# Three weight units converted beside the attention scores with part of the sums on GpSimd, and a reordered stretch from the norms to the first products

## The chip, the cores and the metric

The kernel runs on one core of one Trainium2 chip. The metric is the device time of one execution, in microseconds (us). TensorE multiplies matrices, VectorE and ScalarE work on tiles in SBUF and PSUM, GpSimd works on tiles in SBUF, and SyncE issues the DMAs in the order in which the program lists them. Each engine runs its own instructions strictly in program order and waits for others through semaphores.

## The reference

Channel attention over 6016 tokens of 256 channels, and two feed-forward layers with a hidden size of 2048:

```python
qn = q / (norm(q, axis=tokens) + 1e-6);  kn = k / (norm(k, axis=tokens) + 1e-6)
s = kn.T @ qn / tau                      # 256 x 256, a sum over all 6016 tokens
a = softmax(s, axis=-1)                  # exp(s - max) / (sum + 1e-9)
x = v @ a                                # 6016 x 256
h = x @ w_in1;  x2 = (h * clip(h + 3, 0, 6) / 6) @ w_out1
h = x2 @ w_in2; out = (max(h, 0) ** 2) @ w_out2
```

The four weight matrices arrive as float64 and have to be turned into float32 on the chip.

## The kernel before

**Scores.** The tokens are 47 tiles of 128 rows, loaded as 24 groups (one tile, then two each) into a ring of eight buffers. For each tile `squares` lets ScalarE square q and k into a PSUM bank and VectorE add that to one of two running sums in SBUF, and `score` lets TensorE multiply k by q for the two halves of the 256 x 256 result. For the last ten tiles the second half is put off (`late`): six of those ten scores (`LATE_AT`) come behind the matmuls that finish the norms (`nrm`), the other four behind the broadcast of the reciprocal norms (`rq_ps`).

**Units.** A unit is 512 columns of float64 weights. `from_float64` converts it in five stages: `magnitude` (one ScalarE operation, L154), `sign` (one ScalarE operation, L157, and two VectorE operations, L158 and L159), `high` (VectorE, L162), `low` (VectorE, L167), and `done`, in which `split` lets ScalarE round the value to a high part (L123) and VectorE subtract that to get a low part (L125). All five VectorE operations have their operands in SBUF. Unit 0 of `w_in1` is converted beside the scores; unit 1 is begun ahead of `nrm` and finished in the chain that follows; the others (`order`) follow at places listed in `START` (a place is half a step, below; with k < `DENSE` the five stages stand at consecutive places).

**Chain.** From the norms on: `nrm`, square root, reciprocals, `rq_ps`, per half `softmax`, transposes (`transposed`), and then M1 = (softmax) @ w_in1, 512 columns at a time: `m1_half` are TensorE passes, `m1_out` writes high and low parts of the result as weights, `m1_keep` a float32 copy. `split_first` makes high and low parts of the first tokens of v. `keep_busy` are matmuls on constants whose result nobody reads.

**Steps and the rest.** 32 steps follow for the first 1024 tokens, each six passes for h (`product`), the activation (`first`) and six passes into the accumulators (`second`), with the remaining units, three more parts of M1 and preparations between them. From 154 us on, both layers run in a Strassen scheme whose order is a list of numbered places. Matmuls in full precision are three passes of high and low parts (`passes`, L310 to L312).

Of the kernel before, what the change touches and what calls it, by code (L numbers as in the profile page):

```python
# [8 lines left out]
F32 = mybir.dt.float32  # L9
F32R = mybir.dt.float32r  # L10
I32 = mybir.dt.int32
U32 = mybir.dt.uint32
AF = mybir.ActivationFunctionType
ALU = mybir.AluOpType
AX = mybir.AxisListType

P = 128
C = 256
# [3 lines left out]
KC = C // P  # L22
KF = DFF // P
WIDTHS = [512] * 5 + [448]
NP = len(WIDTHS)
WMAX = max(WIDTHS)
NU = KF // 2
GROUPS = [1] + [2] * 23
DEFER = 10
LATE_AT = 6  # L30
LAG = 2
AHEAD = 3
BUSY = (6, 2, 2, 3)
M1_LEAD = 3
EARLY = 12
TAU_AT = 20
EARLY_AT = {15: (0, 1), 16: (2,), 18: (3, 4)}


START = [-5, -3, 0, 3, 6] + [9 + 4 * k for k in range(9)]  # L40
DENSE = 5
SIGN = -(2 ** 31)
APART = 2.6
APART_FIRST = 3.2
# [2 lines left out]
B11, B21, T2, T3, T1, B22, T4 = range(7)  # L47
# [8 lines left out]
def attention_then_two_ffns(  # L56
# [30 lines left out]
    nc = tc.nc  # L87

    const = ctx.enter_context(tc.tile_pool(name="const", bufs=1))
    wpool = ctx.enter_context(tc.tile_pool(name="wpool", bufs=1))  # L90
    stage = ctx.enter_context(tc.tile_pool(name="stage", bufs=3))
    tpool = ctx.enter_context(tc.tile_pool(name="tpool", bufs=2))
    ops = ctx.enter_context(tc.tile_pool(name="ops", bufs=1))
# [7 lines left out]
    def bank(shape, name, tag=None):  # L101

        if tag is None:
            tag = "yxyq"[turn[0] % 4]
            turn[0] += 1
        return ps_h.tile(shape, F32, tag=tag, name=name, bufs=2 if tag == "y" else 1)
# [13 lines left out]
    def split(hi, lo, x, part=2, eng=nc.vector):  # L120

        if part != 1:
            nc.scalar.copy(hi, x)  # L123
        if part != 0:
            eng.tensor_tensor(out=lo, in0=x, in1=f32(hi), op=ALU.subtract)  # L125
# [47 lines left out]
    wi1, wo1 = {}, {}  # L173
# [4 lines left out]
    def unit(which, u, raw=None):  # L178

        name = f"{which}_{u}"  # L180
        raw = (slot(name) if raw is None else raw).bitcast(I32)
        if which == "wi1":
            c4, k = u // 2, u % 2
            nc.sync.dma_start(out=raw, in_=w_in1[:, k, c4 * 512:(c4 + 1) * 512].bitcast(I32))

            def done(x, part=2):
                if k == 0 and part != 1:
                    wi1[c4] = [
                        spare(2 * c4 + i, f"wi1{s}{c4}", F32R).rearrange("p (k f) -> p k f", k=KC)
                        for i, s in enumerate(("h", "l"))  # L190
                    ]
                split(wi1[c4][0][:, k, :], wi1[c4][1][:, k, :], x, part)
        else:
            nc.sync.dma_start(
                out=raw.rearrange("p (f d) -> p f d", f=2), in_=w_out1[:, 2 * u:2 * u + 2, :].bitcast(I32)
            )

            def done(x, part=2):
                if part != 1:
                    wo1[u] = wo_tile(u, "wo1_")  # L200
                split(wo1[u][:, 0, :], wo1[u][:, 1, :], x, part)

        return from_float64(raw.rearrange("p (d w) -> p d w", w=2), name, done)
# [72 lines left out]
    def small(n):  # L276
        where = next(i for i in range(len(used)) if used[i] + n <= 2 * WMAX)
        at = used[where]
        used[where] += n
        return scratch[where][:, at:at + n]  # L280

    def keep_busy(n, name):

        ps = bank([P, P], name)
        for _ in range(n):
            nc.tensor.matmul(ps, lhsT=ones, rhs=ones, start=True, stop=True)

    s_ps = [ps_acc.tile([P, C], F32, tag="acc", name=f"s{i}") for i in range(KC)]

    sums = [small(2 * C) for _ in range(2)]  # L290
    for x in sums:
        nc.vector.memset(x, 0.0)

    def squares(t, x):
        sq = bank([P, 2 * C], f"sq{t}")
        nc.scalar.activation(sq, x, AF.Square)
        nc.vector.tensor_tensor(out=sums[t % 2], in0=sq, in1=sums[t % 2], op=ALU.add)

    def score(t, x, i):
        nc.tensor.matmul(  # L300
# [13 lines left out]
    with tc.manual_schedule():  # L314
# [8 lines left out]
        pre = []  # L323
        t = 0
        for gi, n in enumerate(GROUPS):
            src = wpool.tile([P, 1024], F32, tag=f"wo{gi % NU}", name=f"qk{gi}")[:, :2 * n * C]
            nc.sync.dma_start(
                out=src.rearrange("p (t x c) -> p t x c", t=n, x=2), in_=qk[:, t:t + n, :, :]
            )
            if gi == EARLY:  # L330
                pre.append(unit("wi1", 0, raw1[0]))
            for st in EARLY_AT.get(gi, ()):
                pre[0][st]()
            if gi == TAU_AT:
                nc.sync.dma_start(out=tau_sb, in_=tau.to_broadcast([P, 1]))
                tq = small(4)
                nc.gpsimd.memset(tq, 1.0)
                nc.gpsimd.tensor_scalar(
                    out=tq[:, 2:4], in0=tq[:, 2:4], scalar1=tau_sb, scalar2=1.0, op0=ALU.mult, op1=ALU.mult
                )  # L340
            for j in range(n):
                x = src[:, j * 2 * C:(j + 1) * 2 * C]
                squares(t, x)
                score(t, x, 0)
                if t < NT - DEFER:
                    score(t, x, 1)
                else:
                    late.append((t, x, 1))
                t += 1
# [1 line left out]
        et = [hpool.tile([P, KC, C], F32R, tag="o", bufs=4, name=f"et{s}") for s in ("h", "l")]  # L351

        order = [
            ("wo1", 0), ("wi1", 2), ("wo1", 1), ("wi1", 3), ("wo1", 2), ("wi1", 4), ("wo1", 3), ("wi1", 5),
            ("wo1", 4), ("wi1", 6), ("wo1", 5), ("wi1", 7), ("wo1", 6), ("wo1", 7),
        ]
        loaded = []

        def feed():
            k = len(loaded)  # L360
            if k < len(order):
                which, u = order[k]
                loaded.append(unit(which, u, raw1[u] if which == "wi1" and u < len(raw1) else None))
# [4 lines left out]
            for k in range(KC):  # L368
                nc.sync.dma_start(out=raw[k][:, :, :w], in_=(vt[p] if j == 0 else x2_d[p])[:, 2 * k:2 * k + 2, :w])

        pre.append(unit("wi1", 1, raw1[1]))
        raw0 = [gpool.tile([P, 2, WMAX], F32, tag="g", name=f"v0_{k}") for k in range(KC)]
        load_x(0, 0, raw0)
        for _ in range(AHEAD):
            feed()


        for st in range(4):
            pre[1][st]()


        nrm = ps_acc.tile([P, 4], F32, tag="acc", name="nrm")
        for b in range(4):
            for m, x in enumerate(sums):
                nc.tensor.matmul(
                    nrm[:, b:b + 1], lhsT=x[:, b * P:(b + 1) * P], rhs=ones[:, 0:1], start=(m == 0), stop=(m == 1)
                )
# [3 lines left out]
        nc.vector.tensor_scalar_max(x2n, nrm, 1e-30)  # L391
        root = small(4)
        nc.scalar.activation(root, x2n, AF.Sqrt, scale=2.0 ** -10)
        pre[1][4](0)
        rec = small(4)
        nc.vector.reciprocal(rec, root)
        half = small(4)
# [5 lines left out]
        nc.vector.reciprocal(rnorm, norm)  # L403

        rq_ps = ps_acc.tile([P, C], F32, tag="acc", name="rq_ps")
        loaded[0][0]()
        for i in range(KC):
            diag = small(P)
            nc.vector.tensor_scalar(out=diag, in0=ident, scalar1=rnorm[:, i:i + 1], scalar2=None, op0=ALU.mult)
            nc.tensor.matmul(rq_ps[:, i * P:(i + 1) * P], lhsT=ones, rhs=diag, start=True, stop=True)  # L410
        for a in late[LATE_AT:]:
            score(*a)
        pre[1][4](1)
        loaded[0][1]()
        nc.scalar.activation(warm, ones[:, 0:1], AF.Exp)
        rq = small(C)
        nc.scalar.copy(rq, rq_ps)

# [24 lines left out]
        def row_sums(i, e, sm, et_ps):  # L443
            rs = const.tile([P, 1], F32, name=f"rs{i}")
            nc.vector.tensor_scalar_add(rs, sm, 1e-9)
            nc.vector.reciprocal(rs, rs)
            rsum.append(rs)
# [4 lines left out]
        def m1_half(c4, i, j):  # L452
            if j == 0:
                mps[c4, i] = bank([P, 512], f"mp{c4}_{i}")
            passes(mps[c4, i], [(
                [t[:, i, j * P:(j + 1) * P] for t in et], [t[:, j, :] for t in wi1[c4]],
            )], j == 0, j == KC - 1)
# [48 lines left out]
            hi, lo = (t[:, u, S1:, :] for t in wa1[c4])  # L506
            split(hi, lo, m1_st[c4][:, u, :, :], part, idle_first(c4 < 2))


        operands = {}  # L510
        raws = {}

        def operand(j, p, r):

            at = j * NP + p
            if r in (B11, B21) and at % 2:
                t = wpool.tile([P, 2, WMAX], F32R, tag=f"b{2 + r}", name=f"x{j}_{p}_{r}")
            elif r == T2 and at % 2:
                t = ops.tile([P, 2, WMAX], F32R, tag="opx", name=f"x{j}_{p}_{r}")
            else:  # L520
                t = ops.tile([P, 2, WMAX], F32R, tag=f"op{r}", name=f"x{j}_{p}_{r}")
            t = t[:, :, :WIDTHS[p]]
            operands[j, p, r] = [t[:, i, :] for i in range(2)]
            return operands[j, p, r]


        x0 = {}

        def split_first(k):
            w = WIDTHS[0]  # L530
            for n in range(2):
                hi, lo = x0[k, n] = operand(0, 0, ((B11, T3), (B21, B22))[k][n])
                split(hi, lo, raw0[k][:, n, :w])

        e0 = softmax(0)
        keep_busy(BUSY[1], "busy1")
        loaded[0][2]()
        transposed(0, *e0)
        e1 = softmax(1)
        loaded[0][3]()  # L540
        loaded[0][4](0)
        rest(0, *e0)
        loaded[0][4](1)
        feed()
        row_sums(0, *e0)
        keep_busy(BUSY[2], "busy2")
        m1_half(0, 0, 0)
        transposed(1, *e1)
        rest(1, *e1)
        row_sums(1, *e1)  # L550
        m1_half(0, 0, 1)
        for k in range(KC):
            split_first(k)
        loaded[1][0]()
        m1_out(0, 0)
        for j in range(KC):
            m1_half(0, 1, j)
        m1_out(0, 1)
        m1_keep(0)
        loaded[1][1]()  # L560
        loaded[1][2]()
        keep_busy(BUSY[3], "busy3")


        x2_d = [dram.tile([P, 4, WMAX], F32, name=f"x2d{p}") for p in range(NP)]
# [408 lines left out]
```

## Time and profile before

| | |
|---|---|
| time, median of 3 runs | 1046.49 us (1046.17 to 1046.52) |
| the profiled execution's own time | 1046.23 us |
| its span, first to last instruction | 1044.1 us |
| busy in the span | TensorE 1033.6, VectorE 863.0, ScalarE 665.6, GpSimd 29.9 us |

The span is 2.1 us shorter than the execution's time, the same execution seen from outside. Times in the rows below count from the start of the span. Matmuls overlap, so that TensorE's progress is read from the starts of its instructions rather than from their durations.

### The profile page before, as it was taken

How to read it: one execution, taken by the hardware profiler on the slowest of the kernel's cores; microseconds unless marked ns; L12 is line 12 of the kernel's file. 1: busy time of each engine (PE TensorE's matmuls, PEld its weight loads, DVE VectorE, ACT ScalarE, POOL GpSimd, SP SyncE). 2: the span in 40 equal slices, each digit the busy share in tenths (PEclk: the TensorE clock that was granted, in tenths of full speed). 3: DMA queues.
4: the chain of work that ended last, by engine and by line, in shares of the span. 5: the costliest groups of instructions: out<-in, count | busy, mean ns of one | idle time of the engine just before them, and what ended most of it. 6: DMA issues, size and time to landing. Idle time of an engine off the chain costs nothing.

```text
span 1044.1 us, 12995 instructions
## 1 busy us (share of the span) xinstructions
PE 1033.6 (99%) x4630; PEld 865.3 (83%) x4630; DVE 863.0 (83%) x1461; ACT 665.6 (64%) x1200; POOL 29.9 (3%) x33
## 2 busy tenths in 40 slices
PE   9999999999999999999999999999999999999998
PEld 8867787888888888888998888888888888888997
DVE  7899868889989989988987788778688678778765
ACT  7687777788878778777876455445455455445443
POOL 0012240000000000000000000000000000000000
PEclk9999999999999999999999999999999999999999
DMA  9911204003403402222665002002001100200100
GB/s 371 344 40 41 81 1 142 1 1 116 157 0 116 156 1 111 82 76 92 227 225 187 1 1 80 1 1 69 13 1 40 42 1 1 75 1 1 41 1 36
DMA packets 25936, 77.64 MB, mean 74 GB/s; under 512 B 2832, under 2 KB 4880, under 8 KB 25872
## 3 DMA queue, kind: packets, MB, share of 16 engines
q1 hardware_dynamic: 25872, 76.82, 21.0%
q8 instruction: 36, 0.59, 0.2%
q14 instruction: 28, 0.23, 0.1%
HBM read 52.95 MB, written 23.86 MB: 74 GB/s over the span
## 4 chain that ended last, share of the span: by engine, by line
PE 88%; DVE 7%; ACT 4%; issue 1%; DMA 1%; SPq 0%; ACTq 0%
PE acc L312 15%; PE acc L311 15%; PE acc L310 15%; PE y L310 7%; PE y L311 7%; PE y L312 7%; PE q L311 4%; PE q L310 4%; PE q L312 4%; PE s L300 3%; PE x L312 2%; PE x L310 2%; PE x L311 2%; DVE gs L125 2%; DVE g L630 1%
## 5 line engine op out<-in xcount | busy, mean ns | idle before, releaser
L125 DVE TENSOR_TENSOR gs<-g,gs 128x512 fp32r<-128x512 f32 (+1 forms) x384 | 260.4, 678 | 55.6 <-ACT gs L793 46.1
L312 PE MATMUL acc<-gs,wo 128*128 128x512 f32 (+1 forms) x768 | 296.8, 386 | 0.8 <-DVE gs L125 0.6
L310 PE MATMUL acc<-gs,wo 128*128 128x512 f32 (+1 forms) x768 | 296.2, 386 | 0.9 <-ACT gs L123 0.9
L311 PE MATMUL acc<-gs,wo 128*128 128x512 f32 (+1 forms) x768 | 295.9, 385 | 0.0
L793 ACT CAST gs<-g 128x512 fp32r<-128x512 f32 (+1 forms) x352 | 208.6, 613 | 31.0 <-DVE g L784 22.0
L312 PEld LDWEIGHTS acc<-gs,wo 128*128 128x128 f32 x768 | 144.2, 188 | 30.8 <-DVE gs L125 4.0
L310 PEld LDWEIGHTS acc<-gs,wo 128*128 128x128 f32 x768 | 144.2, 188 | 28.5 <-ACT gs L123 2.0
L311 PEld LDWEIGHTS acc<-gs,wo 128*128 128x128 f32 x768 | 144.2, 188 | 26.6
L766 ACT COPY se<-y 128x512 f32<-128x512 f32 (+1 forms) x88 | 50.7, 576 | 121.3 <-PE y L312 121.2
L770 DVE TENSOR_TENSOR h<-q,se 128x512 f32<-128x512 f32 (+1 forms) x88 | 59.5, 676 | 63.1 <-ACT se L766 62.6
L766 ACT COPY su<-y 128x512 f32<-128x512 f32 (+1 forms) x88 | 50.7, 576 | 87.1 <-PE y L312 76.4
L789 DVE SCALAR_TENSOR_TENSOR g<-h 128x512 f32<-128x512 f32 (+1 forms) x144 | 97.0, 673 | 0.0
L776 ACT ACTIVATE r<-h,three 128x512 f32<-128x512 f32 (+1 forms) x120 | 85.5, 713 | 8.6 <-DVE h L770 8.2
L784 DVE SCALAR_TENSOR_TENSOR g<-r,h 128x512 f32<-128x512 f32 (+1 forms) x120 | 80.6, 672 | 3.8 <-ACT r L776 3.8
L778 ACT ACTIVATE r<-y 128x512 f32<-128x512 f32 (+1 forms) x48 | 28.3, 590 | 62.7 <-PE y L312 62.7
L770 DVE TENSOR_TENSOR h<-q,su 128x512 f32<-128x512 f32 (+1 forms) x88 | 59.4, 675 | 1.4
L770 DVE TENSOR_TENSOR h<-x,sa 128x512 f32<-128x512 f32 (+1 forms) x88 | 59.1, 672 | 0.0
L766 ACT COPY sa<-y 128x512 f32<-128x512 f32 (+1 forms) x88 | 50.7, 576 | 6.8 <-PE y L312 0.7
L789 DVE SCALAR_TENSOR_TENSOR g<-y,r 128x512 f32<-128x512 f32 (+1 forms) x48 | 32.7, 681 | 23.7 <-ACT r L778 23.1
L300 PE MATMUL s<-qk 128*128 128x256 f32 x188 | 41.7, 381 | 0.8 <-DMA qk<-in_qk 0.8
L300 PEld LDWEIGHTS s<-qk 128*128 128x128 f32 x188 | 35.5, 191 | 6.1 <-DMA qk<-in_qk 1.5
L310 PE MATMUL y<-x,wa_0h 128*128 128x512 f32 (+1 forms) x88 | 34.0, 386 | 0.7 <-ACT se L766 0.7
(241 smaller groups left out, 1761.6 us busy)
## 6 DMA issues: line engine op xcount, KB each, us to landing
qk<-in_qk SPq DMA_DIRECT2D x23, 512.0 KB, 7.0
wo<-in_w_out SPq DMA_DIRECT2D x16, 512.0 KB, 5.2
wi<-in_w_in SPq DMA_DIRECT2D x10, 512.0 KB, 4.6
x2d<-o SPq DMA_DIRECT2D x20, 256.0 KB, 2.4
raw<-x2d SPq DMA_DIRECT2D x10, 512.0 KB, 5.6
out<-o SPq DMA_DIRECT2D x20, 256.0 KB, 2.2
raw<-in_vt SPq DMA_DIRECT2D x8, 512.0 KB, 5.9
wo2d<-wo2s SPq DMA_DIRECT2D x8, 512.0 KB, 2.9
```

The source lines that it names most:

```text
L125: eng.tensor_tensor(out=lo, in0=x, in1=f32(hi), op=ALU.subtract)
L300: nc.tensor.matmul(s_ps[i], lhsT=x[:, C + i * P:C + (i + 1) * P], rhs=x[:, :C], start=(t == 0), stop=(t == NT - 1))
L310: nc.tensor.matmul(ps, lhsT=ah, rhs=bh, start=first, stop=False, skip_group_check=more)
L311: nc.tensor.matmul(ps, lhsT=al, rhs=bh, start=False, stop=False, skip_group_check=more)
L312: nc.tensor.matmul(ps, lhsT=ah, rhs=bl, start=False, stop=last, skip_group_check=more)
L766: nc.scalar.copy(s[tag], s["y"])
L770: nc.vector.tensor_tensor(out=s[which], in0=s[ps], in1=s[tag], op=ALU.add)
L776: nc.scalar.activation(s["r" + which], h, AF.Relu, bias=three)
L778: nc.scalar.activation(s["r" + which], h, AF.Relu)
L784: nc.vector.scalar_tensor_tensor(out=g, in0=s["r" + which], scalar=6.0, in1=h, op0=ALU.min, op1=ALU.mult)
L789: nc.vector.scalar_tensor_tensor(out=g, in0=h, scalar=0.0, in1=r, op0=ALU.max, op1=ALU.mult)
L793: nc.scalar.copy(gs[which][0], s["g" + which])
```

## The change

- The ring for q and k has seven buffers and not eight (wo1 to wo7).
- Three units (0 and 1 of `w_in1`, 0 of `w_out1`) are loaded behind groups 6, 9 and 12 and converted at 3, 3, 4, 5 and 6 groups after their loads; before it was one, loaded behind group 12.
- Every third tile below 39 (1, 4, ..., 37: 13 tiles) is squared into SBUF and added to a third sum by GpSimd. At tile 41 VectorE adds the third sum to the first.
- `split_first(0)` stands ahead of `nrm`; `split_first(1)` is two halves between the softmax and M1. The table load for Exp stands right behind the square root; of the unit stages in the chain, only one `magnitude` is left. Five late scores stand ahead of `rq_ps` and five behind it.
- The transposes of the second half stand ahead of M1's first passes; the last `keep_busy` is gone; `order` and `START` are new.

```diff
-LATE_AT = 6
+LATE_AT = 5
-BUSY = (6, 2, 2, 3)
+BUSY = (6, 2, 2)
-EARLY = 12
+EARLY = ((6, "wi1", 0), (9, "wi1", 1), (12, "wo1", 0))
+EARLY_AT = (3, 3, 4, 5, 6)
-EARLY_AT = {15: (0, 1), 16: (2,), 18: (3, 4)}
+POOL_UNTIL = 39
+JOIN = 41
-START = [-5, -3, 0, 3, 6] + [9 + 4 * k for k in range(9)]
-DENSE = 5
+START = [-1, 2, 5, 8, 11, 14, 17, 22, 26, 30, 34, 39, 45]
+DENSE = 3
...
     def squares(t, x):
-        sq = bank([P, 2 * C], f"sq{t}")
-        nc.scalar.activation(sq, x, AF.Square)
-        nc.vector.tensor_tensor(out=sums[t % 2], in0=sq, in1=sums[t % 2], op=ALU.add)
+        if t % 3 == 1 and t < POOL_UNTIL:
+            sq = hpool.tile([P, 2 * C], F32, tag="r", name=f"sq{t}")
+            nc.scalar.activation(sq, x, AF.Square)
+            nc.gpsimd.tensor_tensor(out=sums[2], in0=sq, in1=sums[2], op=ALU.add)
+        else:
+            sq = bank([P, 2 * C], f"sq{t}")
+            nc.scalar.activation(sq, x, AF.Square)
+            nc.vector.tensor_tensor(out=sums[t % 2], in0=sq, in1=sums[t % 2], op=ALU.add)
+        if t == JOIN:
+            nc.vector.tensor_tensor(out=sums[0], in0=sums[2], in1=sums[0], op=ALU.add)
...
-            src = wpool.tile([P, 1024], F32, tag=f"wo{gi % NU}", name=f"qk{gi}")[:, :2 * n * C]
+            src = wpool.tile([P, 1024], F32, tag=f"wo{1 + gi % (NU - 1)}", name=f"qk{gi}")[:, :2 * n * C]
...
-            if gi == EARLY:
-                pre.append(unit("wi1", 0, raw1[0]))
-            for st in EARLY_AT.get(gi, ()):
-                pre[0][st]()
+            for i, (x, which, u) in enumerate(EARLY):
+                if gi == x:
+                    pre.append(unit(which, u, raw1[u] if which == "wi1" else None))
+                for st, after in enumerate(EARLY_AT):
+                    if gi == x + after:
+                        pre[i][st]()
...
-        pre.append(unit("wi1", 1, raw1[1]))
...
-        for st in range(4):
-            pre[1][st]()
+        split_first(0)
...
         nc.scalar.activation(root, x2n, AF.Sqrt, scale=2.0 ** -10)
-        pre[1][4](0)
+        nc.scalar.activation(warm, ones[:, 0:1], AF.Exp)
+        loaded[0][0]()
...
-        loaded[0][0]()
...
-        pre[1][4](1)
-        loaded[0][1]()
-        nc.scalar.activation(warm, ones[:, 0:1], AF.Exp)
...
         e0 = softmax(0)
         keep_busy(BUSY[1], "busy1")
-        loaded[0][2]()
         transposed(0, *e0)
         e1 = softmax(1)
-        loaded[0][3]()
-        loaded[0][4](0)
+        row_sums(0, *e0)
         rest(0, *e0)
-        loaded[0][4](1)
-        feed()
-        row_sums(0, *e0)
+        split_first(1, 0)
         keep_busy(BUSY[2], "busy2")
-        m1_half(0, 0, 0)
         transposed(1, *e1)
         rest(1, *e1)
         row_sums(1, *e1)
+        m1_half(0, 0, 0)
         m1_half(0, 0, 1)
-        for k in range(KC):
-            split_first(k)
-        loaded[1][0]()
+        split_first(1, 1)
         m1_out(0, 0)
         for j in range(KC):
             m1_half(0, 1, j)
         m1_out(0, 1)
         m1_keep(0)
-        loaded[1][1]()
-        loaded[1][2]()
-        keep_busy(BUSY[3], "busy3")
```

## Rows read from the trace of the kernel before

**Rows 1.** Windows: busy time and count of each engine, clock, DMA share, GB/s.
```profile
7.70:41.60 33.90, 33.90 (x159) 29.87 (x159) 30.77 (x52) 26.90 (x49) 0.70 (x1) 1.00 1.00 378
41.60:55.90 14.30, 12.86 (x72) 10.28 (x70) 11.60 (x32) 10.05 (x22) 0.00 (x0) 1.00 0.67 265
55.90:154.40 98.50, 96.25 (x407) 75.30 (x408) 84.48 (x139) 74.20 (x129) 25.69 (x21) 1.00 0.14 43
...
200.00:300.00 100.00, 100.00 (x442) 82.81 (x442) 92.04 (x160) 79.90 (x142) 0.00 (x0) 1.00 0.21 72
```

**Rows 2.** The chain that ended last, pieces: start, duration, what.
```profile
7.68 33.94 PE s L300 x156
...
45.41 1.28 ACT L415
...
46.91 0.27 ACT scratch L417
```

**Rows 3.** Timeline of the scores: start, duration, instruction, idle before and releaser.
```profile
20.23 0.60 ACT L296 ACTIVATE sq<-qk 128x512 f32<-128x512 f32 x1 [0.15 <-DMA qk<-in_qk]
22.70 0.60 ACT L296 ACTIVATE sq<-qk 128x512 f32<-128x512 f32 x1 [1.35 <-DMA qk<-in_qk]
25.39 0.66 ACT L154 ACTIVATE tbwi<-raw11h 128x512 f32<-128x512 f32 x1
25.94 0.68 ACT L157 ACTIVATE tywi<-raw11h 128x512 int32<-128x512 uint32 x1
26.17 0.42 DVE L158 TENSOR_SCALAR tawi<-raw11h 128x512 int32<-128x512 int32 x1
26.50 0.42 DVE L159 TENSOR_SCALAR tbwi<-tbwi 128x512 f32<-128x512 f32 x1
28.35 0.68 DVE L162 SCALAR_TENSOR_TENSOR tawi<-tbwi,tawi 128x512 int32<-128x512 int32 x1
28.95 0.68 DVE L297 TENSOR_TENSOR scratch<-sq,scratch 128x512 f32<-128x512 f32 x1
31.35 0.68 DVE L167 CUSTOM_DVE_ANT_0 tawi<-tawi,tywi 128x1024 uint16<-128x1024 uint16 x1
32.06 0.62 ACT L123 CAST wi1h<-tawi 128x512 fp32r<-128x512 f32 x1 [2.36 <-DVE tawi L167]
32.59 0.59 ACT L296 ACTIVATE sq<-qk 128x512 f32<-128x512 f32 x1
32.71 0.69 DVE L125 TENSOR_TENSOR wi1l<-tawi,wi1h 128x512 fp32r<-128x512 f32 x1 [0.69 <-ACT wi1h L123]
33.32 7.26 DVE L297 TENSOR_TENSOR scratch<-sq,scratch 128x512 f32<-128x512 f32 x12
```

**Rows 4.** Timeline later on, GpSimd (POOL) and VectorE (DVE) at the same time.
```profile
91.80 0.92 POOL L216 TENSOR_TENSOR m<-m 128x256 f32<-128x256 f32 x1
92.05 0.96 DVE L159 TENSOR_SCALAR tbwi<-tbwi 128x512 f32<-128x512 f32 x1
...
114.63 0.69 DVE L630 SCALAR_TENSOR_TENSOR g<-r,h 128x512 f32<-128x512 f32 x1 [0.90 <-ACT r L628]
114.84 1.30 POOL L125 TENSOR_TENSOR wa_1l<-m,wa_1h 128x512 fp32r<-128x512 f32 x1
115.24 1.46 DVE L167 CUSTOM_DVE_ANT_0 tawo<-tawo,tywo 128x1024 uint16<-128x1024 uint16 x1
```

**Rows 5.** Timeline from the norms to the first product.
```profile
41.24 1.97 PEld L385 LDWEIGHTS nrm<-both,scratch 128*128 128x128 f32 x16
...
45.84 0.61 PE L410 MATMUL rq_ps<-scratch,both 128*128 128x128 f32 x4
...
53.49 0.39 PE L312 MATMUL mp<-wi1l,eth 128*128 128x512 f32 x1
...
54.50 0.47 ACT L476 ACTIVATE wa_0h<-mp,rs 128x256 fp32r<-128x256 f32 x1
...
55.91 0.50 PE L311 MATMUL h<-x,wa_0l 128*128 128x512 f32 x1 [0.38 <-DVE wa_0l L478]
```

More of the change, by code (lines that the diff above doesn't have):

```diff
@@ L288, in attention_then_two_ffns @@
     s_ps = [ps_acc.tile([P, C], F32, tag="acc", name=f"s{i}") for i in range(KC)]
-    sums = [small(2 * C) for _ in range(2)]
+    sums = [small(2 * C) for _ in range(3)]
     for x in sums:
@@ L353, in attention_then_two_ffns @@
         order = [
-            ("wo1", 0), ("wi1", 2), ("wo1", 1), ("wi1", 3), ("wo1", 2), ("wi1", 4), ("wo1", 3), ("wi1", 5),
-            ("wo1", 4), ("wi1", 6), ("wo1", 5), ("wi1", 7), ("wo1", 6), ("wo1", 7),
+            ("wi1", 2), ("wi1", 3), ("wo1", 1), ("wo1", 2), ("wi1", 4), ("wi1", 5), ("wo1", 3), ("wo1", 4),
+            ("wi1", 6), ("wo1", 5), ("wi1", 7), ("wo1", 6), ("wo1", 7),
         ]
@@ L375, in attention_then_two_ffns, with operand, split_first @@
             feed()
-        for st in range(4):
-            pre[1][st]()
+        operands = {}
+        raws = {}
+        def operand(j, p, r):
+            at = j * NP + p
+            if r in (B11, B21) and at % 2:
+                t = wpool.tile([P, 2, WMAX], F32R, tag=f"b{2 + r}", name=f"x{j}_{p}_{r}")
+            elif r == T2 and at % 2:
+                t = ops.tile([P, 2, WMAX], F32R, tag="opx", name=f"x{j}_{p}_{r}")
+            else:
+                t = ops.tile([P, 2, WMAX], F32R, tag=f"op{r}", name=f"x{j}_{p}_{r}")
+            t = t[:, :, :WIDTHS[p]]
+            operands[j, p, r] = [t[:, i, :] for i in range(2)]
+            return operands[j, p, r]
+        x0 = {}
+        def split_first(k, *halves):
+            w = WIDTHS[0]
+            for n in halves or range(2):
+                hi, lo = x0[k, n] = operand(0, 0, ((B11, T3), (B21, B22))[k][n])
+                split(hi, lo, raw0[k][:, n, :w])
+        split_first(0)
         nrm = ps_acc.tile([P, 4], F32, tag="acc", name="nrm")
         for b in range(4):
-            for m, x in enumerate(sums):
+            for m, x in enumerate(sums[:2]):
                 nc.tensor.matmul(
@@ L507, in m1_sums_split @@
             split(hi, lo, m1_st[c4][:, u, :, :], part, idle_first(c4 < 2))
[L510 to L533, printed above, removed]
         e0 = softmax(0)
         keep_busy(BUSY[1], "busy1")
-        loaded[0][2]()
         transposed(0, *e0)
         e1 = softmax(1)
-        loaded[0][3]()
-        loaded[0][4](0)
+        row_sums(0, *e0)
         rest(0, *e0)
-        loaded[0][4](1)
-        feed()
-        row_sums(0, *e0)
+        split_first(1, 0)
         keep_busy(BUSY[2], "busy2")
-        m1_half(0, 0, 0)
         transposed(1, *e1)
```

## The prediction

> **What bounds the kernel now.** I first cut the span into four stretches by the windows view [rows 1]. During the scores (7.7 to 41.6 us) TensorE is busy throughout, and VectorE is busy for 30.8 of 33.9 us: two engines near their limit, TensorE just ahead. The chain of waits [rows 2] says the same: 156 score matmuls without a break, 33.94/156 = 0.2176 us apart. A tile is four of them, 0.87 us; each of the last ten, with half put off, is two, 0.435 us. From 41.6 to 55.9 us the chain goes through all engines in turn (table load, copy of `rq_ps`, and so on). In the steps, 55.9 to 154.4 us, 407 matmuls take 98.5 us; at the undisturbed spacing of 100/442 = 0.2262 us they need 92.1, so TensorE waits some 6.4 us there. From 200 us on nothing is missing [rows 1]; what follows the steps is only shifted. So I ask three things: do the scores still end on time, what does the chain save, and do the steps change?
>
> **Loads.** Groups 12 and 13 were first squared, after a wait for their load, at 20.23 and 22.70 us, with one unit's load between: 2.47 for two loads, 1.24 us per 512 KB [rows 3]. Counting back, group 7 had landed by 14.1; with a unit ahead of it 15.3, while TensorE wants its first tile (13) at 7.68 + 10 x 0.87 = 16.4. Group 10 comes at 20.2 against 21.6, group 13 at 25.2 against 26.8. The seventh-buffer ring issues the last group when tile 32 is scored, at 33.8; landings at 1.24 us per group put it at 37.7, and it is wanted at 40.7. The two loads more are thus hidden by the scores: 0, with at least 1.1 us of cover; without the cover up to 1 us.
>
> **The sums, by counting.** Spacings on VectorE [rows 3]: a sum 0.60 (28.35 to 28.95; twelve in 7.26), L158 0.33, L159 0.33, `high`, `low` and the low part 0.60 to 0.61 each, a unit 2.47. On ScalarE a magnitude 0.55, a sign 0.57, a rounding 0.53 (32.06 to 32.59); I take a square at 0.53 as well, the same size as the rounding. GpSimd's 13 adds remove 13 x 0.60 = 7.8 us from VectorE; the units add 2 x 2.47 plus the join 0.6, all beside the scores. But the help is spread over all tiles, and the units stand in groups 9 to 18. The sum of tile 17 starts at the earliest at 19.3: group 9 lands at 17.7, and its two squares stand behind a magnitude and a sign. From there VectorE owes 23 sums, 13.9, the join 0.6 and 6.75 of unit work (7.41 without the sign just done): 40.6 us if it never waits. `nrm` started at 41.24 [rows 5]. So 0.6 us may be lost.
>
> **The sums, with waits.** Two kinds of wait occur. In the old layout, ScalarE idled 2.36 us until `low` was done and VectorE 0.69 for the rounding [rows 3]; now ScalarE has a magnitude, a sign and two squares queued behind each rounding, and VectorE's sums need those squares. The second kind is in [rows 4]: L167 starts at 115.24, while GpSimd runs 114.84 to 116.14, and takes 1.46 in place of 0.68; L159 at 92.05 ends 0.29 after GpSimd and takes 0.96 in place of 0.42; but L630, which reads one operand from PSUM, takes 0.69 beside GpSimd. So I let VectorE's unit operations and GpSimd's adds exclude each other, first come first served, and leave the sums (PSUM and SBUF) undisturbed. An add is 1.30 us, the row of its size [rows 4].
>
> Laid out by hand in program order: tile 18's sum ends at 20.9. Unit 0: `high` to 21.5; `low` waits for the add of tile 19 until 22.8; the low part for that of tile 22 until 24.7; with the next sign and four sums this ends at 27.2. Unit 1: `high` meets the add of tile 25 (26.9 to 28.2), `low` that of 28 (28.8 to 30.1); ScalarE gets to round only at 30.8, so its next squares start at 32.4; this ends at 34.3. Unit 2: `high` meets the add of 31 (to 35.5), `low` that of 34 (to 37.4); 40.5. Three groups thus take 6.3 to 7.1 us where TensorE needs 5.2. Nine sums and the join follow, 6.05 us from 40.8: 46.9, so `nrm` is 5.7 late. Had `high` of unit 1 come 0.3 us sooner, it would have gone ahead of the add and the rest would end at 45.3, 4.1 late. Without any exclusion the same layout ends at 42.4, 1.2 late. I take the middle of the first two, **+4.9**; bounds 0 (the count above) and 5.7.
>
> [...]
>
> **The chain from `nrm` to the first product**, first on the old clock. Before, `rq_ps` was ready at 45.84 + 0.61 = 46.45, but ScalarE was in the table load (45.41 to 46.69) and the copy stands at 46.91 in the chain [rows 2, 5]. Now the table load runs 43.75 to 45.03 and the one magnitude ends at 45.7; five late scores end at 45.33, `rq_ps` is ready at 45.95, copied at 46.0: -0.8 for the first half. The second half needs the five other scores, 45.95 + 10 x 0.2176 plus drain = 48.3, so that it gains only about 0.3. Its exponential stands behind the first rounding of the transposes (49.0 to 49.35), so its transposes end at 50.55, and M1's twelve passes, without waits, at 50.55 + 12 x 0.2262 = 53.27; before it was 53.49 + 0.23 = 53.72 [rows 5]. Now comes the larger part: before, `m1_out` waited on ScalarE behind four roundings of v and a magnitude until 54.50, and the products got going at 55.91 - 0.23 = 55.68 [rows 5]. With two roundings ahead of the norms and two in gaps, `m1_out` runs at 52.1, its low part ends at 53.43, and the products start at 53.27, their second pass at 53.5. **-2.4**; bounds -0.5 (M1 alone) and -3. The roundings ahead of the square root cost nothing while `nrm` runs (1.97 us for 2 x 0.60 on VectorE, 2 x 0.53 on ScalarE). With `keep_busy` six matmuls go, in time in which TensorE waited anyway: 0.
>
> **Steps.** 13 units remain where 12 and the last two stages of a thirteenth did: sign and `high` more, 1.3 us of VectorE among 84.5 [rows 1]. Per step VectorE needs 1.3 for activation and low part and TensorE 12 x 0.2262 = 2.71, so a unit (2.47) per three places asks 1.3 + 1.65 per step, 0.2 too much; one per four places fits. The old order was dense up to place 13, the new one is lighter up to place 10 and dense to 22. I expect some 1 us less waiting at first and as much more afterwards: **0**, bounds -1.5 and +1.5.
>
> **Sum**, against the profiled execution: 1046.23 (span 1044.1 and 2.1 around it) + 4.9 - 2.4 + 0 = 1048.7. The median of the runs is 0.26 above that execution: **1049.0**.
>
> **Rivals.** (1) The exclusion costs next to nothing, since unit operations fall into GpSimd's gaps: `nrm` 1.2 late, 1046.49 + 1.2 - 2.4 = 1045.3. For it: GpSimd is idle half the time. Against: in [rows 4] both operations of a unit were blocked in full. (2) The sums end on time, TensorE ends the scores as before, and the chain's saving stands alone: 1044.1, or 1042.6 with the steps' lower bound. It needs VectorE to lose under 0.6 us in 21; from that point each microsecond lost is one on the end. (3) TensorE idles nearly 5 us ahead of `nrm`, longer than at any place of the old trace, and runs at half rate afterwards; five late scores ahead of `rq_ps` would then take 2.2 us more: 1051.2. [...]
>
> **How the numbers follow.** Forecast 0.48, on its own 1047.0 to 1050.2; rival 1 0.22; rival 2 0.15; rival 3 0.15. A measurement tells about 0.2% from no change, 2.1 us: 1044.4 to 1048.6 counts as the same. Of the forecast 0.33 lies above that and 0.15 within; rival 3 is slower; rival 1 is within, but for 0.03; rival 2 is faster. Faster 0.18, same 0.34, slower 0.48. The range 1043.8 to 1052.4 leaves out half of rival 2 and the top of rival 3, with the loads' extra microsecond.
>
> **What would show it.** Right: `nrm` starts near 46 us and not at 41.2, behind VectorE's sums; TensorE has a gap just ahead of it; VectorE's L162, L167 or L125 in 20 to 38 us are often 1.0 us and longer; the first product follows `nrm`'s start by 12.0 us and not 14.4; 98 to 99 us lie between it and the first Strassen pass. Wrong: `nrm` near 41 to 42 us; score matmuls with gaps that a load ends (then the ring is too short); or a first stretch of the steps with far less waiting than 6 us in all. What I trust least is whether each unit operation meets an add: a few tenths of shift in the squares change who comes first.

## The result: slower by 0.9%

The changed kernel takes 1056.03 us (median of 4 runs, 1054.28 to 1057.16), the kernel before 1046.51 in the same comparison: a ratio of 1.009, 95% interval 1.0078 to 1.0102. That is 9.5 us more, where 2.5 were forecast and the range ended at 1052.4. The profiled execution has a span of 1054.8 us, 10.7 more than before.

The windows view of the changed kernel, in the four stretches of [rows 1] (bounds moved to its own first product and its first Strassen pass):

```profile
7.70:41.60 33.90, 33.59 (x156) 29.56 (x156) 28.91 (x43) 27.61 (x51) 16.64 (x14) 1.00 0.99 387
41.60:60.20 18.60, 14.67 (x67) 12.44 (x65) 10.77 (x29) 9.04 (x20) 0.00 (x0) 0.82 0.47 193
60.20:165.20 105.00, 99.66 (x410) 77.70 (x409) 87.01 (x140) 74.67 (x129) 26.00 (x22) 0.97 0.13 41
165.20:1054.80 889.60, 884.72 (x3973) 744.89 (x3971) 732.92 (x1235) 551.27 (x996) 1.69 (x2) 1.00 0.18 62
```

The last stretch is as long as it was. The second is 4.5 us longer and the third 6.3, counted from the start of undisturbed products: before, that start was at 55.68 us, counted back from the second pass in [rows 5], and the first Strassen pass came 98.7 us later. And the granted clock, the third number from the right, is no longer 1.00 in these two. Narrower windows show where:

```profile
45.30:52.70 7.40, 7.38 (x27) 6.48 (x28) 2.67 (x10) 2.25 (x4) 0.00 (x0) 0.54 0.68 277
103.60:107.40 3.80, 3.80 (x12) 2.94 (x11) 3.03 (x6) 2.97 (x6) 0.00 (x0) 0.55 0.09 35
134.50:138.20 3.70, 3.70 (x10) 2.86 (x10) 3.69 (x8) 2.31 (x4) 0.00 (x0) 0.54 0.00 0
```

Three times the granted clock fell to half: it is 0.50 from 46.3 to 52.7, from 104 to 107 and from 135 to 138 us, and the windows above hold a little at 1.00 besides. The 128x512 passes start 0.43 us apart in the second of them (104.41, 104.84, 105.27) and 0.23 ahead of it (103.28, 103.51, 103.74). So I let a stretch at a mean clock of c do c of its work; by this estimate TensorE fell behind by 7.4 x 0.46 = 3.4, 3.8 x 0.45 = 1.7 and 3.7 x 0.46 = 1.7 us in them. Whether that lengthens the whole depends on the next wait, as the experiments show.

The timeline of the scores, VectorE (DVE) and GpSimd (POOL), and what follows (L167 and L172 here are `high` and `low`, L130 the low part, L307 a sum):

```profile
22.33 1.01 DVE L172 CUSTOM_DVE_ANT_0 tawi<-tawi,tywi 128x1024 uint16<-128x1024 uint16 x1
23.08 1.41 POOL L303 TENSOR_TENSOR scratch<-sq,scratch 128x512 f32<-128x512 f32 x1 [0.28 <-ACT sq L302]
24.03 1.00 DVE L130 TENSOR_TENSOR wi1l<-tawi,wi1h 128x512 fp32r<-128x512 f32 x1
...
32.76 1.27 POOL L303 TENSOR_TENSOR scratch<-sq,scratch 128x512 f32<-128x512 f32 x1 [2.37 <-ACT sq L302]
32.78 1.80 DVE L167 SCALAR_TENSOR_TENSOR tawo<-tbwo,tawo 128x512 int32<-128x512 int32 x1
34.33 1.39 POOL L303 TENSOR_TENSOR scratch<-sq,scratch 128x512 f32<-128x512 f32 x1 [0.29 <-ACT sq L302]
35.11 1.15 DVE L172 CUSTOM_DVE_ANT_0 tawo<-tawo,tywo 128x1024 uint16<-128x1024 uint16 x1
...
42.19 3.08 DVE L307 TENSOR_TENSOR scratch<-sq,scratch 128x512 f32<-128x512 f32 x5
...
45.32 2.98 PEld L422 LDWEIGHTS nrm<-both,scratch 128*128 128x128 f32 x16 [3.78 <-DVE scratch L307]
48.25 4.61 PE L312 MATMUL s<-qk 128*128 128x256 f32 x10
52.65 0.65 PE L447 MATMUL rq_ps<-scratch,both 128*128 128x128 f32 x4
```

What answers to [rows 3]: of the nine operations of the three units that took 0.68 each, six (four are shown) take 1.0 to 1.8 us, each ending 0.5 to 0.6 after a GpSimd add does; the last five sums end at 45.3; TensorE, done with its scores at 41.95, waits 3.4 us and starts `nrm` at 45.32; before, its weight loads began at 41.24 [rows 5] and its matmuls at 41.46. Then it is slow: the weight loads of `nrm` spread over 2.98 us and not 1.97, and the ten records of five late scores start over 4.4 us, up to `rq_ps`, where 10 x 0.2176 = 2.2 was their rate.

In the steps, the same view around the second half-rate stretch:

```profile
96.29 1.29 POOL L130 TENSOR_TENSOR wa_0l<-m,wa_0h 128x512 fp32r<-128x512 f32 x1 [1.18 <-ACT wa_0h L128]
96.33 1.79 DVE L172 CUSTOM_DVE_ANT_0 tawi<-tawi,tywi 128x1024 uint16<-128x1024 uint16 x1
97.53 1.19 POOL L221 TENSOR_TENSOR m<-m 128x256 f32<-128x256 f32 x1
98.81 1.26 DVE L130 TENSOR_TENSOR wi1l<-tawi,wi1h 128x512 fp32r<-128x512 f32 x1
99.49 1.19 POOL L221 TENSOR_TENSOR m<-m 128x256 f32<-128x256 f32 x1
100.00 0.96 DVE L163 TENSOR_SCALAR tawo<-wo 128x512 int32<-128x512 int32 x1
100.64 0.90 POOL L221 TENSOR_TENSOR m<-m,m 128x256 f32<-128x256 f32 x1
100.88 0.94 DVE L164 TENSOR_SCALAR tbwo<-tbwo 128x512 f32<-128x512 f32 x1
102.48 0.50 PE L324 MATMUL acc<-gs,wo 128*128 128x512 f32 x1 [1.85 <-DVE gs L130]
...
133.89 0.50 PE L322 MATMUL mp<-wi1h,eth 128*128 128x512 f32 x1 [1.66 <-ACT wi1h L128]
```

The four VectorE operations shown take 1.79, 1.26, 0.96 and 0.94 us beside GpSimd's own work on M1's weights, where those of a unit in the kernel before, at 98.4 to 103 us with GpSimd idle, take 0.69, 0.68, 0.42 and 0.42; an operation of the activation between them, which reads one operand from PSUM, takes 0.67 us at 98.05. TensorE waits 1.85 us for a low part of the activation and is at half rate from about 103.6. The last row is the wait ahead of the third half-rate stretch.

### The profile page after: what moved, and what is told of

It reads as the page before. It is cut to its first block, busy times and chain, and to the rows that moved or that the text cites. A ratio compares the mean times of both kernels' runs of the same rounds, so it can differ in the third digit from the quotient of the medians.

```text
span 1054.8 us, 12972 instructions
## 1 busy us (share of the span) xinstructions
PE 1038.7 (98%) x4624; PEld 869.8 (82%) x4624; DVE 862.5 (82%) x1450; ACT 665.8 (63%) x1200; POOL 46.5 (4%) x46
## 4 chain that ended last, share of the span: by engine, by line
PE 91%; DVE 4%; ACT 2%; DMA 1%; issue 1%; SPq 0%; ACTq 0%; DVEq 0%
PE acc L324 16%; PE acc L322 16%; PE acc L323 16%; PE y L322 7%; PE y L323 7%; PE y L324 7%; PE q L322 4%; PE q L324 4%; PE q L323 4%; PE x L324 2%; PE x L322 2%; PE x L323 2%; DMA qk<-in_qk 1%; PE s L312 1%; PE h L323 1%; PE h L324 1%
## 5 line engine op out<-in xcount | busy, mean ns | idle before, releaser
L130 DVE TENSOR_TENSOR gs<-g,gs 128x512 fp32r<-128x512 f32 (+1 forms) x384 | 261.1, 680 | 57.7 <-ACT gs L792 46.1
L765 ACT COPY su<-y 128x512 f32<-128x512 f32 (+1 forms) x88 | 50.7, 577 | 87.4 <-PE y L324 75.0
L312 PE MATMUL s<-qk 128*128 128x256 f32 x188 | 44.2, 397 | 0.9 <-DMA qk<-in_qk 0.9
```

What stands on the lines that cost most here:

```text
L312: nc.tensor.matmul(s_ps[i], lhsT=x[:, C + i * P:C + (i + 1) * P], rhs=x[:, :C], start=(t == 0), stop=(t == NT - 1))
L765: nc.scalar.copy(s[tag], s["y"])
```

## Experiments

The theory after the result had three parts. GpSimd's adds hold up VectorE's unit operations, so the sums come late. TensorE's pause ahead of the norms is what halves its rate. In the steps, the new places of the units meet GpSimd's operations there, and the waits halve the rate again. Rivals: ScalarE's waits and the loads make the sums late; the rate falls without a pause; the new places are too dense, whatever GpSimd does. Intervals below are 95%, against the kernel before on the same chip.

**e1: the pause filled.** Fourteen products of constants ahead of `nrm`.

```diff
+        keep_busy(14, "busyn")
         nrm = ps_acc.tile([P, 4], F32, tag="acc", name="nrm")
```

> 28 more matmul records on constants fill TensorE's pause ahead of the norms; nothing else changes. If the pause ahead of the norms is what halves TensorE's rate, the norms and the five late scores run at the full rate again (the stretch from the start of nrm to rq_ps 4.3 us and not 7.3), the first product comes about 3.2 us earlier, and the whole is about 1052.8 us. If the rate falls for another reason, nrm still takes 3 us, and the time stays at 1056.

Measured: 1053.21 us, ratio 1.0069 (1.0052 to 1.0085). The filler had to wait 1.80 us for a PSUM bank and put `nrm` off to 46.40, but the granted clock of the stretch around it is 1.00 again:

```profile
43.17 3.39 PE L291 MATMUL busyn<-both 128*128 128x128 f32 x28 [1.80 <-DVE scratch L307]
```
```profile
41.40:57.80 16.40, 14.07 (x92) 12.88 (x93) 10.59 (x29) 8.90 (x20) 0.00 (x0) 1.00 0.50 201
```

From `nrm` to `rq_ps` it is 3.9 us, from `nrm` to the first product (57.82) 11.4, where the changed kernel took 7.3 and 14.8. So with matmuls in the pause the clock stayed at 1.00, and the half-rate stretch cost 3.4 us there. The first product came 2.3 us earlier and not 3.2, because the filler put `nrm` off. The time came out near the expected 1052.8 partly by luck: another 1.6 us fell away in the steps, where the wait at 131.61 was not followed by half rate this time.

**e2: no adds.** GpSimd's adds are left out, so 13 of the 47 tiles are missing in the norms.

```diff
-            nc.gpsimd.tensor_tensor(out=sums[2], in0=sq, in1=sums[2], op=ALU.add)
```

> The 13 adds on GpSimd are left out (the squares are taken, but the norms lack a third of the tiles). If the adds hold up VectorE's unit operations, those take 0.4 to 0.7 us each again, the sums end at about 42.4 us, nrm starts about 1.2 us later than before the change and not 4.1, TensorE's pause shrinks below 1 us and its rate doesn't fall: about 7 us less than the changed kernel by the first product, so 1049 us with the steps as they are. If the wait of ScalarE for VectorE or later loads made the sums late, nrm still starts near 45 us and the time stays above 1054.

Measured: 1049.72 us, ratio 1.0032 (1.0021 to 1.0043). The unit operations take 0.68 again, and `nrm` starts at 43.43:

```profile
22.06 0.68 DVE L172 CUSTOM_DVE_ANT_0 tawi<-tawi,tywi 128x1024 uint16<-128x1024 uint16 x1
...
26.52 0.63 ACT L302 ACTIVATE sq<-qk 128x512 f32<-128x512 f32 x1 [0.95 <-DMA qk<-in_qk]
27.67 0.69 DVE L306 TENSOR_TENSOR scratch<-sq,scratch 128x512 f32<-128x512 f32 x1 [0.70 <-ACT sq L305]
...
43.43 2.83 PEld L421 LDWEIGHTS nrm<-both,scratch 128*128 128x128 f32 x16 [1.91 <-DVE scratch L306]
```

So in these two profiles the adds account for 1.9 of the 4.1 us; 2.2 are there without any blocking, one more than expected. Part of that one is a load: the group of tiles 25 and 26, forecast for 25.2, is squared at 26.52 after a wait of 0.95, and VectorE waits 0.70 for a square behind it. The split is rough: the profiles of the changed kernel, e1, e3 and e4, alike on VectorE up to there, end their sums at 45.3, 44.9, 45.8 and 45.7. The expectation of the rate failed in the profiled execution: it fell to 0.55 all the same (43.4 to 50.7 us) after a pause of 1.5 us. That execution took 1054.13 us, the slowest of eight; four others took 1048.4 to 1049.0 at a higher mean clock (0.998 against 0.996), and where their rate fell isn't on record.

**e8: the adds alone** in the kernel before, with the join.

```diff
-        sq = bank([P, 2 * C], f"sq{t}")
...
+        if t % 3 == 1 and t < 39:
...
+            nc.gpsimd.tensor_tensor(out=sums[2], in0=sq, in1=sums[2], op=ALU.add)
```

> The kernel before with GpSimd's 13 adds and the join alone: one early unit, nothing else moved. Five unit operations can meet an add, at most some 4 us of waiting, against 7.2 us of VectorE relieved: the sums still end ahead of TensorE, nrm starts at 41.2 to 41.5, and the time is that of before, 1046.2. If the adds hurt by themselves, nrm comes over 1 us late here too.

Measured: 1046.57 us, ratio 0.9999 (0.999 to 1.0008). `nrm` starts at 41.83, 0.6 late and 0.3 past what was expected. With one unit beside the scores the adds don't change the time, although two operations of that unit were held up (1.32 and 1.63 us); with three units and no adds `nrm` is 2.2 late; with both, 4.1. The profiled execution was the slowest of ten (1048.05), and its rate fell behind `nrm`, though no wait is listed for the matmuls there and 0.53 us for their weight loads:

```profile
41.83 1.95 PE L392 MATMUL nrm<-both,scratch 128*128 128x1 f32 x16
```
```profile
44.00:48.00 4.00, 4.00 (x13) 3.22 (x11) 2.68 (x11) 3.32 (x6) 0.00 (x0) 0.57 0.98 387
```

So the rate can fall without a pause like that of the changed kernel.

**e4: late scores in the pause**, seven ahead of `nrm`, three behind it, none behind `rq_ps`.

```diff
+        for a in late[:7]:
+            score(*a)
         nrm = ps_acc.tile([P, 4], F32, tag="acc", name="nrm")
...
-        for a in late[:LATE_AT]:
+        for a in late[7:]:
...
-        for a in late[LATE_AT:]:
-            score(*a)
```

> Seven of the late scores are moved ahead of nrm, into the pause, and three stand behind it, none behind rq_ps. By the theory of the pause, rate and waiting are both cured there: nrm still starts near 45.3 us, takes 1.9, rq_ps comes 3 us earlier than in the changed kernel, and the first product near 56.5 instead of 60.2: 1052. If the pause isn't what halves the rate, about 2 us less come of the scores alone, with nrm still at 3 us: 1054.

Measured: 1053.37 us, ratio 1.0063 (1.0047 to 1.0079). `nrm` took 1.9 us again behind a wait of 1.74, and `rq_ps` came 3.0 us earlier (49.60). But the rate fell 2.7 us after `nrm` had begun, among the last three late scores, and stayed at half through most of the chain, in which TensorE now often waits for other engines; the first product came at 59.61 and not 56.5. The scores in the pause moved the half-rate stretch and didn't cure it:

```profile
50.00:58.00 8.00, 6.59 (x23) 5.43 (x23) 4.24 (x12) 3.55 (x11) 0.00 (x0) 0.50 0.02 5
```

**e3: units at even places.**

```diff
-START = [-1, 2, 5, 8, 11, 14, 17, 22, 26, 30, 34, 39, 45]
+START = [-1, 2, 6, 10, 14, 18, 22, 26, 30, 33, 36, 41, 46]
```

> Only the places of the units in the steps are changed, from one unit per three places up to place 22 to one per four. If the density of the units there makes TensorE wait in the steps, the stretch from the first product to the first Strassen pass falls from 105 us to some 100 (the old 98.7), without the fall to half rate near 100 us: 1051. If it is GpSimd's own work there that holds up VectorE, the waits near 100 and 132 us stay within 1 us of what they were, and so does the time, 1055 to 1056.

Measured: 1058.98 us, ratio 1.0118 (1.0103 to 1.0133), worse. It decides nothing about density: its places finish the last input unit right ahead of M1's last part, and that part waits 3.80 us for it, 2.1 us more than in the changed kernel. My choice of places made that wait longer.

```profile
135.96 0.80 PE L322 MATMUL mp<-wi1h,eth 128*128 128x512 f32 x1 [3.80 <-ACT wi1h L128]
```

**e5: old order and places in the steps**, on top of e1.

```diff
-            ("wi1", 2), ("wi1", 3), ("wo1", 1), ("wo1", 2), ("wi1", 4), ("wi1", 5), ...
+            ("wi1", 2), ("wo1", 1), ("wi1", 3), ("wo1", 2), ("wi1", 4), ("wo1", 3), ...
-START = [-1, 2, 5, 8, 11, 14, 17, 22, 26, 30, 34, 39, 45]
-DENSE = 3
+START = [-1, 0, 3, 6, 9, 13, 17, 21, 25, 29, 33, 37, 41]
+DENSE = 4
```

> On top of the filler matmuls ahead of the norms (e1, 1053.2 us), the units in the steps stand in the old order and, but for the first two, at the old places. If the new order and places make the steps longer, the stretch from the first product to the first Strassen pass falls from 103 us to 99 or 100, with no fall to half rate in it: 1049.5. If what makes them longer is where GpSimd's operations now meet VectorE's, whatever the order, it stays at 102 or more and the time above 1052.

**e6: GpSimd reads nothing in the steps**, on top of e1; memsets take the place of its sums and subtractions.

```diff
-        eng.tensor_tensor(out=b(st, to), in0=x, in1=y, op=op)
+        if eng is nc.gpsimd:
+            nc.gpsimd.memset(b(st, to), 0.5)
+        else:
+            eng.tensor_tensor(out=b(st, to), in0=x, in1=y, op=op)
```

> On top of e1, GpSimd's sums and subtractions in the steps (parts of M1's weights, and the preparation of the second 1024 tokens) are replaced by memsets of the same tiles, so that it reads nothing: these operands hold constants. If GpSimd's reading is what blocks VectorE there, no VectorE operation of a unit takes over 1 us in the steps any more, TensorE's waits near 97 to 100 and 130 us shrink by some 3 us together, and its rate doesn't fall there: 1049 to 1050. If the unit places alone load VectorE too densely, the waits stay and the time is 1052 or more.

**e10: both.**

> e5 and e6 together: the old order and places of the units, and memsets for GpSimd's operations that read, in the steps (the operands named in e6 hold constants). If the two are separate costs, the stretch from the first product to the first Strassen pass falls below e6's 96.8 us by e5's 3.6, to 93. If the new places cost only by meeting GpSimd's operations, it is 96 to 97 with either order, and the time that of e6, 1046.7.

Measured: e5 1049.58 us (1.0034, 1.0021 to 1.0046), e6 1046.75 (1.0007, 0.9998 to 1.0016), e10 1045.31 (0.9995, 0.9985 to 1.0004). e5 came as expected; e6 fell more than 2 us below its own expectation of 1049 to 1050. The windows view of e1, e5, e6 and e10, one row each, from the first product to the first Strassen pass:

```profile
57.82:161.23 103.41, 98.02 (x409) 76.48 (x408) 86.08 (x139) 73.96 (x128) 25.14 (x21) 0.98 0.14 41
```
```profile
57.21:157.03 99.82, 97.13 (x409) 75.13 (x408) 84.51 (x140) 74.73 (x129) 24.77 (x21) 1.00 0.14 43
```
```profile
57.81:154.62 96.81, 95.63 (x410) 75.51 (x409) 79.75 (x140) 74.50 (x129) 9.75 (x23) 1.00 0.15 44
```
```profile
57.34:152.93 95.59, 94.19 (x410) 76.03 (x408) 79.88 (x140) 74.99 (x129) 9.48 (x23) 1.00 0.14 45
```

e1 has one half-rate stretch there, in which TensorE fell 1.7 us behind. The profiles of e2 and e4 have the same instructions in the steps, e2 without any half rate there and e4 with the same single stretch; they take 103.35 and 103.41 us:

```profile
58.30:161.65 103.35, 97.28 (x410) 75.11 (x408) 86.08 (x139) 74.01 (x128) 24.67 (x21) 1.00 0.13 41
```
```profile
128.08 0.50 PE L323 MATMUL acc<-gs,wo 128*128 128x512 f32 x1 [1.71 <-DVE gs L130]
131.98 0.50 PE L321 MATMUL mp<-wi1h,eth 128*128 128x512 f32 x1 [0.62 <-ACT wi1h L128]
```
```profile
131.61 0.50 PE L322 MATMUL mp<-wi1h,eth 128*128 128x512 f32 x1 [1.67 <-ACT wi1h L128]
```

The first two are of e2 (windows, then timeline), the last is of e1. M1's last part waits for its unit and starts 73.7 to 73.8 us after the first product in e2, in e1 and in the changed kernel; what TensorE lost at half rate before, it would otherwise have waited. So the first half-rate stretch in the steps cost nothing in the end, and the second, behind that wait, 1.6 us (105.0 against 103.4).

The four are thus to be compared as they stand. GpSimd's reads cost 6.6 us with the new places and 4.2 with the old, and VectorE's busy time is 6.3 and 4.6 lower without them; the new places cost 3.6 with the reads and 1.2 without. The medians of the times say the same: 6.5 and 4.3, 3.6 and 1.4 (the intervals of e6 and e10 overlap, so that the last is not clear of the noise). Neither expectation of e10 held (93, or the same as e6); 95.6 is nearer the second. Some two thirds of what the new places cost comes of meeting GpSimd's operations. The memsets are also shorter than what they replace (GpSimd is busy for 9.8 us in place of 25.1), so that e6 doesn't separate the reads from GpSimd's results coming earlier; that VectorE's own operations got shorter speaks for the reading. The reads were there before the change as well; what the change added in the steps are its places, which meet them more dearly, and the half rate that followed a longer wait.

**e7: the reordered chain alone**, with the scores of the kernel before, and **e9**, the same with the unit for M1's second part moved ahead of an output unit. Of their edits, the table load and e9's places:

```diff
+        nc.scalar.activation(warm, ones[:, 0:1], AF.Exp)
         pre[1][4](0)
...
-START = [-5, -3, 0, 3, 6] + [9 + 4 * k for k in range(9)]
+START = [-5, -1, 2, 5, 8, 10] + [13 + 4 * k for k in range(8)]
```

> The scores of the kernel before (one early unit, eight buffers, all sums on VectorE), with the reordered chain: table load behind the square root, roundings of v into gaps, transposes ahead of M1's passes, the first unit's stages in VectorE's gaps, two stages more left to the steps. If the chain's saving is real by itself, nrm starts at 41.2 and the first product at about 53.8 us and not 55.7; a little is given back in the steps: 1045.0. If the chain gains only because the units' work was taken out of it, the first product comes at 55 us or later and the time is 1046 or more.

> As e7, but the unit that the second part of M1 waits for (wi1, 3) is converted ahead of the output unit (wo1, 1), at places 2 to 6. If e7 lost its chain's gain in the 2.06 us wait ahead of M1's second part, that wait shrinks to 0.9 as in the kernel before, and the time is some 1.2 us under e7's 1046.65, 1045.4. If the gain is used up by VectorE's work in the steps anyway, the wait turns up at another place and the time stays at 1046.3 to 1046.7.

Measured: e7 1046.65 us (1.0002, 0.9994 to 1.001), e9 1046.00 (0.9997, 0.9988 to 1.0006). e7's profile can't decide about the chain: it shows the slowest of twelve executions (1049.34), with a half-rate stretch behind `nrm`, and the first product at 55.17. In e9's the rate holds, the first product comes at 53.60, 2.1 us earlier than before, and the steps take 101.0 and not 98.7:

```profile
53.60:154.57 100.97, 97.85 (x410) 74.83 (x408) 85.79 (x142) 75.71 (x131) 24.73 (x21) 1.00 0.13 42
```

What the chain saves, the steps give back: e9 is no faster within its interval, and no version here beats the kernel before beyond it. VectorE is busy for 1.1 us more in these steps (85.8 against 84.7 from 55.68 on); that this is why they are 2.3 longer isn't shown. Between the two expectations of e9 the 1046.0 doesn't decide; TensorE's wait ahead of M1's second part did shrink from 1.67 us in e7 to 0.52, as before (0.49).

## Why the prediction was wrong

**The sums: the mechanism right, the size partly by luck.** `nrm` was forecast 4.9 us late, the middle of two layouts (4.1 and 5.7), and came 4.1 late by its weight loads (3.9 by its matmuls), behind VectorE's sums; as forecast, six operations of units were blocked. It took the course of the first layout, in which `high` of unit 1 goes ahead of the add: it started at 26.88, the add at 27.20. But that layout had 1.2 without blocking and 2.9 from it, where e2 leaves 2.2 and 1.9: two errors of 1 us that cancel. The loads stayed hidden: the scores took 33.94 us as before and ended 0.3 later, as they had begun 0.3 later. Their cover was thinner than worked out, since tiles 25 and 26 landed at 26.4 and not 25.2.

**The chain: right at the full rate.** -2.4 was forecast; from `nrm`'s first matmul on it was 14.2 us before (41.46 to 55.68) and 11.4 in e1, -2.8.

**The pause: priced as a rival where it was a consequence.** The forecast itself had TensorE idle for nearly 5 us, and gave half rate a chance of 0.15 and 2.2 us, since no row of before had such a pause. The rate fell and cost 3.4: the five scores 2.2 as priced, and `nrm` itself 1.2, which I had left out.

**The steps: the step that failed.** "0, bounds -1.5 and +1.5" counted VectorE's work per place at its undisturbed durations. The exclusion that the prediction had read from the very same stretch [rows 4] was applied to the scores and not to the steps. They became 6.3 us longer. Of that, e5 ascribes 3.6 to the new order and places; without GpSimd's reads the same places cost 1.2, which would have been within the bounds. Another 1.6 is the half-rate stretch behind the wait at 133.89; the prediction had priced half rate behind `nrm` alone. The remaining 1.1 is near the 1.3 us of VectorE work that the prediction saw move into the steps and priced at nothing; that it is this work isn't shown. With the other terms as they came out, a 0 here would have given some 1051, within the stated range.

**Put together**, by TensorE's starts: 3.9 for `nrm` (41.46 to 45.32), -2.8 for the chain and 3.4 for half rate in it (both by e1), 4.7 for the steps without the second half-rate stretch there and 1.6 for it: 10.8, which is the 10.7 between the spans but for rounding. The terms cut up that one difference, so that the sum has to come out; what the experiments show is the split.

What stays open: why the rate fell after some short pauses and not after others. In e2's profile a wait of 1.84 us in the steps passed without it, in the changed kernel one of 1.85 didn't; the wait for M1's last part was 1.67 in e1 and 1.66 in the changed kernel, and only the second was followed by half rate. Each of these readings is of a single execution, and the four runs of the changed kernel are 2.9 us apart.

## What to carry to other kernels

Before work goes to GpSimd beside a busy VectorE, count which VectorE operations have all their operands in SBUF and let each of GpSimd's that reads hold one up for its rest (beside the scores here until 0.5 to 0.6 us past the end of an add, 1.0 to 1.8 us in place of 0.68), in every stretch where both occur. A pause of TensorE costs more than its length when the clock falls behind it (a wait of 3.4 us and 3.4 more at 0.50 in the changed kernel); price it with the half rate of what comes next, but only up to the next point at which TensorE would have waited anyway. Shortening a serial chain pays only if the stretch behind it doesn't owe the same engine the work that was taken out.

## What was not expected of the hardware

- The clock fell at pauses far shorter than the 3.4 us of the changed kernel. In the profile of e7, its slowest run of twelve, `nrm`, 16 matmuls of one column, stood behind a wait of 0.4 us, and the granted clock was 0.72 from 42 to 48 us; in e8's no wait is listed, and it was 0.57 from 44 to 48; in the kernel before it stayed at 1.00 through the same matmuls:

```profile
42.00:48.00 6.00, 6.00 (x30) 5.22 (x31) 4.55 (x14) 2.50 (x5) 0.00 (x0) 0.72 0.93 382
```

- A half-rate stretch ahead of a wait for another engine can be free: of two that set TensorE back by 1.7 us each, the first changed nothing in the end and the second cost 1.6.
- GpSimd's memsets of the same tiles did not hold up VectorE as its sums did: in e6, `low` takes 0.69 us on average in the steps, in the changed kernel 0.87 for the input units.
